# Convolution in groups of five blocks instead of four, with the weights staged in a group buffer and the exponential's table loaded first

## The chip, the core and the metric

The kernel runs on one core of a Trainium2 chip. The core has five engines, each with its own in-order instruction queue: PE (TensorE, matrix products; its weight loads are listed apart as PEld), DVE (VectorE), ACT (ScalarE), POOL (GpSimd) and SP (SyncE, which here only starts DMA transfers). PE writes to PSUM, an accumulator memory of eight banks, and a bank can be used again only after another engine has copied its result out, which is called eviction here. All other operands lie in SBUF, the on-chip working memory. The metric is the device time of one execution in microseconds (us); smaller is better.

## The reference

The computation is a short causal convolution over the sequence followed by a maxout layer. Each of 8 heads (24 of the 192 channels each) has 7 taps, normalised by a softmax; then come three products with 192x768 weights, an elementwise maximum and one product back.

```python
B, S, D = x.shape                 # 8, 4160, 192
w = weight - np.max(weight, axis=-1, keepdims=True)      # 8 heads x 7 taps
w = np.exp(w)
w = w / (np.sum(w, axis=-1, keepdims=True) + 1e-09)
...
out = np.einsum('hk,bskhg->bshg', w, x_unf)              # 7 taps, causal
...
h = np.maximum(np.maximum(x @ w1, x @ w2), x @ w3)       # 768 hidden columns
return (h @ w_out).astype(np.float32)
```

## The kernel before

**Blocks and steps.** The 33,280 tokens are cut into NB = 65 blocks of 512. After a hand-ordered front (lines 677 to 726), the main loop (line 747) runs one step per block t, from 2 to 64. A step does the first layer of block t (`l1`, L503, six columns j of 128 hidden units), the second layer of block t - 1 (`st2`, L567), and feeds later blocks: it loads their rows, casts them, and convolves them.

**The maximum.** The weights are stored as differences w1 - w3 and w2 - w3 (`make_wd`, L302), so a column needs two sets of products, `lp` (PSUM pool psp, two banks) and `lq` (pool psq, two banks). `top` turns them into the hidden value: ACT computes r = relu(lp) (L490), then DVE takes max(r, lq) (L491). The missing w3 part goes straight to the output through a small matrix m16 (`make_m`). The second layer accumulates in `po` (pool psw, four banks), and ACT and DVE add its two halves (L574, L575).

**Two lanes.** Contractions of 192 are cut into pieces of 64 rows, and PE holds two such pieces at a time, one in each half of its rows. The two lanes are queues of recorded products (`mm`, `emit`); `emit` interleaves them by the number of columns that each has streamed. `meet` empties both lanes before work that needs all rows. On the chip the result is one in-order PE queue.

**The convolution.** For block 4 on, the rows of x (fp32, buffers `xf`) are cast by POOL to fp16 into a group tile x16 (`cast_x`, L194), which holds the blocks of a group side by side. `conv` (L357) multiplies them with a band matrix (`band`) built from the 7 taps: for each head, four column blocks and two row halves, a 39x32 product whose width is 48 columns per block of the group: 48 for the single block 4, 96 for the pairs 5 to 12, 192 for the groups of four from block 13 (QUADS) on. The results G use two psw banks, one psp and one psq bank (WPWQ). `evac` (L397) evicts them to `ys`: ACT the two psw banks, then DVE the psp bank and the psq bank. `turn` (L411) transposes two blocks at a time by DMA from SP's queue into a tile `yp`, and `double` (L420, POOL) copies it to the other half of the partitions, since each lane reads its own half.

**When it happens.** `convs_at` names the steps that hold a convolution, called late steps: a pair is convolved in one step, a group of four in two halves of four heads, in the steps t - 4 and t - 3 for a group starting at block t. The burst stands after column j = 1, behind a `meet`. `OWN` and `AHEAD` give the lanes unequal numbers of second-layer products ahead of it, so that both end together. `casts` and `loads` say up to which block a step casts and loads; from block 11 on, the loads use three `xf` buffers in turn.

**The front.** SP issues the loads of block 0, the weights in pieces (`ws`, `w3s`), and blocks 1 to 3. ACT loads the 8x7 taps and computes their exponential (L269), which needs a function table; DVE normalises it into `line` (L274); PE turns `line` into the band (L283), which ACT and DVE evict (L287). Blocks 0 to 3 use another convolution (`conv_dense`, L378) with their rows cast into `xz` (L211), by DVE for block 0, by POOL and ACT for block 1. `keep_warm` (L252) issues products without use, to keep PE active.

Of the kernel before, what the change touches and what calls it, by code (L numbers as in the profile page):

```python
# [10 lines left out]
FP32 = mybir.dt.float32  # L11
FP16 = mybir.dt.float16
AXX = mybir.AxisListType.X
AF = mybir.ActivationFunctionType

P = 128
KW = 7
PAD = KW - 1
NHEAD = 8
GRP = 24  # L20
BAND_W = 128 + PAD
# [7 lines left out]
def kernel(  # L29
# [12 lines left out]
    nc = tc.nc  # L42
# [5 lines left out]
    DFF = moe_w1.shape[1]  # L48
# [9 lines left out]
    for b in range(B):  # L58
        s = nfull * NBLK
        while s < SEQ:  # L60
            n = min(SEQ - s, NBLK - off)
# [8 lines left out]
    NB = len(blocks)  # L70
# [15 lines left out]
    NDENSE = 4  # L86
# [12 lines left out]
    const = ctx.enter_context(tc.tile_pool(name="const", bufs=1))  # L99
    x16p = ctx.enter_context(tc.tile_pool(name="x16p", bufs=2))  # L100
    x16q = ctx.enter_context(tc.tile_pool(name="x16q", bufs=2))
    ysp = ctx.enter_context(tc.tile_pool(name="ysp", bufs=2))
    ydp = ctx.enter_context(tc.tile_pool(name="ydp", bufs=4))
    ypp = ctx.enter_context(tc.tile_pool(name="ypp", bufs=4))
    rp = ctx.enter_context(tc.tile_pool(name="rp", bufs=4))
    hp = ctx.enter_context(tc.tile_pool(name="hp", bufs=2))
    tp = ctx.enter_context(tc.tile_pool(name="tp", bufs=2))
# [2 lines left out]
    psp = ctx.enter_context(tc.tile_pool(name="psp", bufs=2, space=bass.MemoryType.PSUM))  # L110
    psq = ctx.enter_context(tc.tile_pool(name="psq", bufs=2, space=bass.MemoryType.PSUM))
    psw = ctx.enter_context(tc.tile_pool(name="psw", bufs=4, space=bass.MemoryType.PSUM))

    QUADS = 13
    assert (NB - QUADS) % 4 == 0
    xin, xbuf, XBUF, loaded = {}, [], 7, set()

    def get_x(t):
# [52 lines left out]

    pairs = {NDENSE: (NDENSE, 0, 1)}
    for t in range(NDENSE + 1, NB):
        u = (t - NDENSE - 1) % 2 if t < QUADS else (t - QUADS) % 4
        pairs[t] = (t - u, u, 2 if t < QUADS else 4)

    def place(t):
        return pairs.get(t, (t, 0, 0))
# [3 lines left out]
    def cast_x(t):  # L182
        if not 0 <= t < NB:
            return
        xf, p0, _ = xin.pop(t)
        t0, u, nu = place(t)
        if u == 0:
            pool = x16q if nu == 4 else x16p
            x16s[t0] = pool.tile([P, NHEAD, 4, nu, 2, GRP], FP16, tag="x16", name=f"x16_{t0}")
        if p0:  # L190
            nc.gpsimd.memset(xf[0:p0, 0, :], 0.0)
        K = HALF + KR
        for r in range(2):
            nc.gpsimd.tensor_copy(out=x16s[t0][0:K, :, :, u, r, :].rearrange("p h j c -> p j h c"),  # L194
                                  in_=xf[0:K, 4 * r:4 * r + 4, :].rearrange("p j (h c) -> p j h c", c=GRP))

    NC, NSLOT, CYC = D // HALF, D // 32, 96
# [16 lines left out]

    ws = const.tile([P, NC, DFF], FP32)
    w3s = const.tile([P, 2, DFF], FP32)
    PW = 2 * P

    def load_wa(f):
# [6 lines left out]

    wk = const.tile([NHEAD, KW], FP32)
    nc.scalar.dma_start(out=wk[:], in_=weight)  # L230
    wos = const.tile([P, NJ, D], FP32)
    load_x(0)
    load_wa(slice(0, PW))
# [14 lines left out]
    def keep_warm(n, pool=psw, tag="w"):  # L248

        ps = pool.tile([P, NBLK], FP32, tag=tag, name="idle")  # L250
        for _ in range(n):
            nc.tensor.matmul(ps[:], lhsT=idle[:, 0:P], rhs=idle[:], start=True, stop=True)  # L252
# [6 lines left out]
    nc.vector.memset(line[:], 0.0)  # L259
    for v in range(2):  # L260
        nc.vector.memset(xz[0][v][:], 0.0)
    band = const.tile([P, NHEAD, BAND_W], FP16)
    nc.vector.memset(band[:], 0.0)
    keep_warm(5, psp, "p")
    wexp = const.tile([NHEAD, KW + 1], FP32)
    nc.vector.memset(wexp[:], 1e-9)
    wneg = const.tile([NHEAD, 1], FP32)
    nc.vector.reduce_max(out=wneg[:], in_=wk[:], axis=AXX, negate=True)
    nc.scalar.activation(out=wexp[:, 0:KW], in_=wk[:], func=AF.Exp, bias=wneg[:])  # L269
    wrec = const.tile([NHEAD, 1], FP32)  # L270
    nc.vector.reduce_sum(out=wrec[:], in_=wexp[:], axis=AXX)
    nc.vector.reciprocal(out=wrec[:], in_=wrec[:])
# [6 lines left out]
    for lo, hi, copy in ((0, CUT, nc.scalar.copy), (CUT, WIN, nc.vector.tensor_copy)):  # L279
# [6 lines left out]
        for a in range(4):  # L286
            copy(out=band[32 * a:32 * a + 32, :, 32 * a + lo:32 * a + hi],  # L287
                 in_=bps[:, 0:hi - lo, :].rearrange("p c h -> p h c"))
# [102 lines left out]
    def evac(t, i, copy=nc.scalar.copy):  # L391
        if t >= NB:
            return
        G, h0 = convs[t]
        per = G[i].shape[1]
        h0 += per * (i // 2)
        copy(out=slots[t][:, i % 2, :, :, GRP * h0:GRP * (h0 + per)].rearrange(  # L397
                 "p u r (h c) -> p h (u r) c", c=GRP),
             in_=G[i][:].rearrange("p h (n c) -> p h n c", c=GRP))

    def turn(t, vs=(0,)):


        nu = place(t)[2]
        for v in vs:
            n = min(nu, 2)
            yp = ypp.tile([P, 2, 2, n, NC, P], FP16, tag="yp", name=f"yp_{t + v}")
            for u in range(n):
                dense[t + v + u] = yp
            for i in range(2):  # L410
                nc.sync.dma_start_transpose(out=yp[:, 0, i, :, :, :].rearrange("p u k n -> p (u k) n"),  # L411
                                            in_=slots[t][:, i, v:v + n, :, :].rearrange("p u r d -> p (u r d)"))

    def double(t):

        if not NDENSE <= t < NB:
            return
        yp = dense[t]
        for i in range(2):
            nc.gpsimd.tensor_copy(out=yp[HALF * i:HALF * (i + 1), 1, :, :, :, :].rearrange("p i u k n -> p (i u k n)"),  # L420
                                  in_=yp[HALF * (1 - i):HALF * (2 - i), 0, :, :, :, :].rearrange("p i u k n -> p (i u k n)"))

    def spot(t, i, c, r):

        _, u, nu = place(t)
        u, nu = u % 2, min(nu, 2)
        f = NC * (r % 2) + c
        return (((f % 2 != i) * 2 + r // 2) * nu + u) * NC + f // 2

# [27 lines left out]
    def op(fn):  # L457
        ops.append((tuple(put), fn))
# [21 lines left out]
    def meet():  # L480

        emit(True)
        assert not ops
        clock[0] = clock[1] = 0
# [244 lines left out]

    convs_at = {2: 4, 3: 5, 4: 7}  # L730
    convs_at.update({t - 3: t for t in range(9, QUADS, 2)})
    convs_at.update({t - 4 + i: t for t in range(QUADS, NB, 4) for i in range(2)})
    casts = {4: 9}
    for t in range(5, NB):
        casts[t] = min(NB - 1, casts[t - 1] + (2 if t in (6, 7, 8) else 1))
    loads = {t: min(NB - 1, casts.get(t + 1, 0) + (t < 7 or t > 9)) for t in range(4, NB)}
    loads.update({2: 9, 3: 10})

    def load_on(t):
        for v in range(loads[t - 1] + 1, loads[t] + 1):  # L740
            if v not in loaded:
                load_x(v)
# [4 lines left out]
    for t in range(2, NB):  # L747
        u = convs_at.get(t, NB)
        late = t > 2 and u < NB
        if t in (3, 4):  # L750
            double(t + 1)
        if t > 3:
            for v in range(casts.get(t - 1, 8) + 1, casts[t] + 1):
                cast_x(v)
        l1(t, 0)
        if t == 2:
            first_rest()
        elif t == 3:
            cast_x(8)
            nc.gpsimd.tensor_copy(out=m16[0:HALF, 2, :], in_=m16[HALF:P, 0, :])  # L760
            nc.gpsimd.tensor_copy(out=m16[HALF:P, 2, :], in_=m16[HALF:P, 1, :])
        if t > 3 and not late:
            op(lambda t=t: (store(t - 2, 0, 4, (nc.sync,)),
                            turn(t + 2, (2,)) if place(t + 2)[1:] == (0, 4) else None, load_on(t)))
        else:
            op(lambda t=t: store(t - 2, 0, 4, (nc.sync,)))
        cuts = ROOM if late else EVEN
        st2(t - 1, (cuts[0], cuts[0]))
        for j in range(1, NJ):
            l1(t, j)  # L770
            if late and j == 1:
                st2(t - 1, (cuts[0] + OWN + AHEAD, cuts[0] + OWN))
                meet()
                quad, second = u >= QUADS, u < QUADS or t == u - 3
                conv(u, WPWQ, range(4 * second, 4 * second + 4) if quad else range(NHEAD))
                for i in (0, 2):
                    evac(u, i)
                for i in (1, 3):
                    evac(u, i, nc.vector.tensor_copy)
                if second:  # L780
                    turn(u)
                load_on(t)
            if t == 2 and j == 1:
                meet()
                conv_dense(3, (ACT, DVE))
                zero_x(1, NQ, NR, nc.vector)
                cross(3, GP)
                load_x(8)
                cast_x(6)
            elif t == 2 and j == 3:  # L790
                meet()
                conv(u, WW)
                evac(u, 0)
                evac(u, 1, nc.vector.tensor_copy)
                turn(4)
                load_x(9)
                cast_x(7)
            st2(t - 1, (cuts[j], cuts[j]))
            if j == 1 and t > 4 and t + 2 in pairs and pairs[t + 2][1] % 2 == 0:
                double(t + 2)  # L800
            if t == NB - 1 and j == 3:
                op(lambda: store(NB - 2, 0, 2, (nc.sync,)))
        if t == NB - 1:
            op(lambda: store(NB - 2, 2, 4, (nc.sync,)))
# [29 lines left out]
```

## Time and profile before

| | us |
|---|---|
| median of 3 runs | 454.24 |
| lowest and highest run | 454.09, 456.25 |
| the profiled execution: its time | 454.51 |
| the profiled execution: span from the first to the last instruction | 452.7 |

The page that the profiler gives for one execution has busy times per engine, the chain of work that ended last (followed back from the last instruction, at each step to what released it), and the costliest groups of instructions. A group names its source line, engine, operation, the tile written and the tiles read, the shape, how often it ran, its total busy time in us and the mean duration of one in ns; then comes the idle time of the engine just before these instructions and what ended it. A timeline row has the start (us from the first instruction), the duration from the first start to the last end of the merged instructions, and then the same names; in brackets stands the idle time before it and its releaser. Rows of the chain are start, duration, and what ran. Durations of overlapping instructions on one engine include the overlap.

| | before |
|---|---|
| L567, 64x192 second-layer products | 3744, 243 ns each |
| L503, 64x512 first-layer products | 2232, 376 ns each |
| L357, convolution products, width 192, 96, 48 | 832, 256, 64 |
| L397, evictions of 384 columns, ACT | 61, 482 ns each |
| L397, evictions of 384 columns, DVE | 61, 550 ns each |
| L411, DMA transposes on SP's queue | 62, median 1280 ns to issue |
| L420, doublings on POOL: 64x1536, 64x768 | 60 at 1465 ns, 2 at 825 ns |
| L630 and L614, DVE evictions of 192 and 384 columns | 358 and 551 ns |

Each product is listed with its latency; two products of one lane follow each other at a shorter distance than the listed duration.

### The profile page before, as it was taken

What the parts mean: (1) busy time and instruction counts of PE and PEld (TensorE: products, weight loads), DVE (VectorE), ACT (ScalarE), POOL (GpSimd) and SP (SyncE); (2) the same over time, 40 slices, a digit from 0 to 9 for tenths busy, and PEclk for the clock granted to TensorE, in tenths of its full rate; (3) what the DMA queues carried; (4) which work ended last, traced back from release to release, by engine and by line L of the source; (5) the groups of instructions that cost most, each with busy time, mean ns of one, the idle gap of its engine ahead of it and who ended that gap; (6) DMA issues with size and microseconds to landing.
All of it is one profiled execution on the core that took longest, in us unless ns stands there. A gap on an engine that the chain in (4) does not pass through costs nothing.

```text
span 452.7 us, 18493 instructions
## 1 busy us (share of the span) xinstructions
PE 446.8 (99%) x7702; PEld 412.6 (91%) x7702; DVE 356.5 (79%) x617; ACT 320.0 (71%) x604; POOL 202.9 (45%) x226
## 2 busy tenths in 40 slices
PE   7999999999999999999999999999999999999997
PEld 3569999999999999999999999999999999999996
DVE  7768778878878787887878788887878788787775
ACT  7767767767777676777767777776767777776664
POOL 2864836556454534645263464535346452505000
PEclk9999999999999999999999999999999999999999
DMA  7969997596875869587685949657594776535223
GB/s 205 231 178 166 199 205 195 146 206 180 169 180 147 168 129 207 138 176 185 118 190 141 210 117 184 177 136 186 133 206 124 178 189 118 117 89 104 59 72 106
DMA packets 127987, 72.03 MB, mean 159 GB/s; under 512 B 52064, under 2 KB 127711, under 8 KB 127903
## 3 DMA queue, kind: packets, MB, share of 16 engines
q1 hardware_dynamic: 127743, 70.75, 68.3%
q8 instruction: 60, 0.98, 1.0%
q14 instruction: 24, 0.20, 0.1%
q10 hardware_dynamic: 160, 0.10, 0.1%
HBM read 33.28 MB, written 25.56 MB: 130 GB/s over the span
## 4 chain that ended last, share of the span: by engine, by line
PE 97%; ACT 1%; DMA 0%; DVE 0%; issue 0%; ACTq 0%
PE po L567 36%; PE lq L503 31%; PE lp L503 22%; PE G L357 3%; PE lw L526 1%; PE lp L526 1%; PE D L378 1%; PE po L625 0%; PE po L598 0%; DMA wk<-in_weight_dram 0%; PE lq L526 0%; ACT xf L137 0%; ACT band L287 0%; ACT L269 0%; PE pm L337 0%; PE band L283 0%
## 5 line engine op out<-in xcount | busy, mean ns | idle before, releaser
L491 DVE TENSOR_TENSOR h<-r,lq 128x512 f16<-128x512 f16 x384 | 263.0, 686 | 85.1 <-ACT r L490 77.3
L567 PE MATMUL po<-wo,h 64*128 64x192 f16 x3024 | 329.8, 243 | 0.0
L490 ACT ACTIVATE r<-lp 128x512 f16<-128x512 f32 x384 | 229.0, 597 | 114.3 <-PE lp L503 100.8
L503 PE MATMUL lp<-yp,wd 64*128 64x512 f16 x1098 | 295.6, 376 | 0.0
L503 PE MATMUL lq<-yp,wd 64*128 64x512 f16 x1098 | 295.5, 376 | 0.0
L567 PEld LDWEIGHTS <-h 64*128 64x128 f16 x3024 | 240.9, 94 | 6.3 <-issue 4.1
L503 PEld LDWEIGHTS <-wd 64*128 64x128 f16 x2268 | 177.7, 94 | 10.6 <-issue 0.2
L194 POOL CAST x<-xf 103x768 f16<-103x768 f32 x122 | 97.5, 827 | 106.6 <-DMA xf<-in_x_dram 93.0
L567 PE MATMUL po<-m,yp 64*128 64x192 f16 x720 | 141.0, 243 | 0.0
L420 POOL COPY yp<-yp 64x1536 f16<-64x1536 f16 (+1 forms) x62 | 89.6, 1445 | 96.2 <-DMA yp<-ys 75.9
L575 DVE TENSOR_TENSOR o<-a,po 128x384 f32<-128x384 f32 x126 | 69.0, 547 | 0.0
L567 PEld LDWEIGHTS <-yp 64*128 64x128 f16 x720 | 66.3, 94 | 0.5
L574 ACT COPY a<-po 128x384 f32<-128x384 f32 x126 | 59.5, 472 | 0.0
L397 ACT CAST ys<-G 128x384 f16<-128x384 f32 x61 | 26.3, 482 | 9.5 <-PE G L357 9.4
L397 DVE CAST ys<-G 128x384 f16<-128x384 f32 x61 | 31.0, 550 | 0.0
L357 PE MATMUL G<-x,band 39*32 39x192 f16 (+2 forms) x1152 | 17.3, 234 | 0.0
L357 PEld LDWEIGHTS <-band 39*32 39x32 f16 x1152 | 10.7, 91 | 5.2 <-issue 4.7
L503 PE MATMUL lp<-yd,wd 64*128 64x512 f16 x36 | 9.7, 376 | 0.0
L503 PE MATMUL lq<-yd,wd 64*128 64x512 f16 x36 | 9.7, 376 | 0.0
L526 PEld LDWEIGHTS <-wd 128*128 128x128 f16 (+1 forms) x48 | 3.2, 98 | 5.7 <-issue 2.4
L211 POOL CAST xz<-xf 112x160 f16<-112x160 f32 (+2 forms) x15 | 4.1, 319 | 7.7 <-DMA xf<-in_x_dram 7.7
L378 PEld LDWEIGHTS <-xz 112*32 112x32 f16 x320 | 4.6, 107 | 2.7 <-issue 1.0
(74 smaller groups left out, 98.2 us busy)
## 6 DMA issues: line engine op xcount, KB each, us to landing
xf<-in_x_dram SPq DMA_DIRECT2D x113, 234.0 KB
out_dram<-o SPq DMA_DIRECT2D x62, 384.0 KB
xf<-in_x_dram SPq DMA_DIRECT2D x7, 204.8 KB
xf<-in_x_dram SPq DMA_DIRECT2D x3, 420.0 KB
ws<-in_moe_w_dram SPq DMA_DIRECT2D x8, 128.0 KB
yp<-ys SPq DMA_TRANSPOSE x62
out_dram<-o SPq DMA_DIRECT2D x5, 192.0 KB
wos<-in_moe_w_out_dram SPq DMA_DIRECT2D x1, 576.0 KB
```

The costliest lines, as they stand in the source:

```text
L194: nc.gpsimd.tensor_copy(out=x16s[t0][0:K, :, :, u, r, :].rearrange("p h j c -> p j h c"), in_=xf[0:K, 4 * r:4 * r + 4, :].rearrange("p j ( ...
L357: nc.tensor.matmul(G[2 * (k // per) + i][TOK * j:TOK * (j + 1), k % per, :], lhsT=band[row, h, HALF * i + LAP:HALF * i + KR], rhs=x16s[t0] ...
L378: nc.tensor.matmul(ps[32 * g:32 * g + 32, lo:hi], lhsT=xz[t][v][0:rlen, q, 32 * s:32 * s + 32], rhs=band[0:rlen, h, cc:cc + hi - lo], star ...
L397: copy(out=slots[t][:, i % 2, :, :, GRP * h0:GRP * (h0 + per)].rearrange("p u r (h c) -> p h (u r) c", c=GRP), in_=G[i][:].rearrange("p h ...
L420: nc.gpsimd.tensor_copy(out=yp[HALF * i:HALF * (i + 1), 1, :, :, :, :].rearrange("p i u k n -> p (i u k n)"), in_=yp[HALF * (1 - i):HALF * ...
L490: nc.scalar.activation(out=r[:], in_=ps[0][:], func=AF.Relu)
L491: nc.vector.tensor_max(out=hs[t][:, j, :], in0=r[:], in1=ps[1][:])
L503: nc.tensor.matmul(ps[i][:], lhsT=w_of(i, c, j), rhs=y_all(t, i, c), start=(n == 0), stop=(n == NC - 1))
L526: nc.tensor.matmul(open_ps[t, j, i][:], lhsT=a, rhs=b, start=(t, j, i) not in begun, stop=(t, j, i) in begun)
L567: nc.tensor.matmul(ps[b0, i][:, s % 2, :], lhsT=a, rhs=b, start=first, stop=last)
L574: nc.scalar.copy(out=a[:], in_=ps[s - 1, 0][:])
L575: nc.vector.tensor_add(out=outs[t][:, s - 1:s + 1, :], in0=a[:], in1=ps[s - 1, 1][:])
```

## The change

From block 15 on, groups hold five blocks (NU = 5): the products are 240 columns wide and a group tile holds five blocks. Blocks 13 and 14 become a pair, so there are five pairs (5 to 14) and ten groups of five instead of four pairs and thirteen groups of four. A late half now evicts 480 columns per bank. The fifth block of a group is transposed alone, in the step before the group (`turn(t + 1, (4,))`), into a `yp` tile of its own, and doubled alone; `spot` gives its places. `ypp` has five buffers instead of four. Step 9 has no convolution any more and casts two blocks instead of one, and the late steps 9 and 10 of the first group become 11 and 12, behind the pair's step 10.

The staged weights `ws` and `w3s` become slices of one tile `wall`, which is taken from the pool of the group tiles (x16q, two buffers) instead of standing on its own for the whole kernel.

In the front a 1x1 exponential is issued on ACT right behind the load of the taps, so that the function table is loaded there; its DVE memset stands first in DVE's queue. The memset of `band` and the idle products move behind the exponential of the taps.

```diff
--- before.py
+++ after.py
@@ -101,7 +101,7 @@
     x16q = ctx.enter_context(tc.tile_pool(name="x16q", bufs=2))
     ysp = ctx.enter_context(tc.tile_pool(name="ysp", bufs=2))
     ydp = ctx.enter_context(tc.tile_pool(name="ydp", bufs=4))
-    ypp = ctx.enter_context(tc.tile_pool(name="ypp", bufs=4))
+    ypp = ctx.enter_context(tc.tile_pool(name="ypp", bufs=5))
     rp = ctx.enter_context(tc.tile_pool(name="rp", bufs=4))
     hp = ctx.enter_context(tc.tile_pool(name="hp", bufs=2))
     tp = ctx.enter_context(tc.tile_pool(name="tp", bufs=2))
@@ -111,8 +111,8 @@
     psq = ctx.enter_context(tc.tile_pool(name="psq", bufs=2, space=bass.MemoryType.PSUM))
     psw = ctx.enter_context(tc.tile_pool(name="psw", bufs=4, space=bass.MemoryType.PSUM))
 
-    QUADS = 13
-    assert (NB - QUADS) % 4 == 0
+    QUADS, NU = 15, 5
+    assert (NB - QUADS) % NU == 0
     xin, xbuf, XBUF, loaded = {}, [], 7, set()
 
     def get_x(t):
@@ -171,8 +171,8 @@
 
     pairs = {NDENSE: (NDENSE, 0, 1)}
     for t in range(NDENSE + 1, NB):
-        u = (t - NDENSE - 1) % 2 if t < QUADS else (t - QUADS) % 4
-        pairs[t] = (t - u, u, 2 if t < QUADS else 4)
+        u = (t - NDENSE - 1) % 2 if t < QUADS else (t - QUADS) % NU
+        pairs[t] = (t - u, u, 2 if t < QUADS else NU)
 
     def place(t):
         return pairs.get(t, (t, 0, 0))
@@ -185,7 +185,7 @@
         xf, p0, _ = xin.pop(t)
         t0, u, nu = place(t)
         if u == 0:
-            pool = x16q if nu == 4 else x16p
+            pool = x16q if nu == NU else x16p
             x16s[t0] = pool.tile([P, NHEAD, 4, nu, 2, GRP], FP16, tag="x16", name=f"x16_{t0}")
         if p0:
             nc.gpsimd.memset(xf[0:p0, 0, :], 0.0)
@@ -214,8 +214,8 @@
 
 
 
-    ws = const.tile([P, NC, DFF], FP32)
-    w3s = const.tile([P, 2, DFF], FP32)
+    wall = x16q.tile([P, NC + 2, DFF], FP32, tag="x16", name="wall")
+    ws, w3s = wall[:, 0:NC, :], wall[:, NC:NC + 2, :]
     PW = 2 * P
 
     def load_wa(f):
@@ -228,6 +228,9 @@
 
     wk = const.tile([NHEAD, KW], FP32)
     nc.scalar.dma_start(out=wk[:], in_=weight)
+    warm = const.tile([1, 1], FP32)
+    nc.vector.memset(warm[:], 0.0)
+    nc.scalar.activation(out=warm[:], in_=warm[:], func=AF.Exp)
     wos = const.tile([P, NJ, D], FP32)
     load_x(0)
     load_wa(slice(0, PW))
@@ -259,14 +262,14 @@
     nc.vector.memset(line[:], 0.0)
     for v in range(2):
         nc.vector.memset(xz[0][v][:], 0.0)
-    band = const.tile([P, NHEAD, BAND_W], FP16)
-    nc.vector.memset(band[:], 0.0)
-    keep_warm(5, psp, "p")
     wexp = const.tile([NHEAD, KW + 1], FP32)
     nc.vector.memset(wexp[:], 1e-9)
     wneg = const.tile([NHEAD, 1], FP32)
     nc.vector.reduce_max(out=wneg[:], in_=wk[:], axis=AXX, negate=True)
     nc.scalar.activation(out=wexp[:, 0:KW], in_=wk[:], func=AF.Exp, bias=wneg[:])
+    band = const.tile([P, NHEAD, BAND_W], FP16)
+    nc.vector.memset(band[:], 0.0)
+    keep_warm(5, psp, "p")
     wrec = const.tile([NHEAD, 1], FP32)
     nc.vector.reduce_sum(out=wrec[:], in_=wexp[:], axis=AXX)
     nc.vector.reciprocal(out=wrec[:], in_=wrec[:])
@@ -403,7 +406,7 @@
 
         nu = place(t)[2]
         for v in vs:
-            n = min(nu, 2)
+            n = min(nu - v, 2)
             yp = ypp.tile([P, 2, 2, n, NC, P], FP16, tag="yp", name=f"yp_{t + v}")
             for u in range(n):
                 dense[t + v + u] = yp
@@ -423,7 +426,7 @@
     def spot(t, i, c, r):
 
         _, u, nu = place(t)
-        u, nu = u % 2, min(nu, 2)
+        u, nu = u % 2, min(nu - u + u % 2, 2)
         f = NC * (r % 2) + c
         return (((f % 2 != i) * 2 + r // 2) * nu + u) * NC + f // 2
 
@@ -729,10 +732,10 @@
 
     convs_at = {2: 4, 3: 5, 4: 7}
     convs_at.update({t - 3: t for t in range(9, QUADS, 2)})
-    convs_at.update({t - 4 + i: t for t in range(QUADS, NB, 4) for i in range(2)})
+    convs_at.update({t - 4 + i: t for t in range(QUADS, NB, NU) for i in range(2)})
     casts = {4: 9}
     for t in range(5, NB):
-        casts[t] = min(NB - 1, casts[t - 1] + (2 if t in (6, 7, 8) else 1))
+        casts[t] = min(NB - 1, casts[t - 1] + (2 if t in (6, 7, 8, 9) else 1))
     loads = {t: min(NB - 1, casts.get(t + 1, 0) + (t < 7 or t > 9)) for t in range(4, NB)}
     loads.update({2: 9, 3: 10})
 
@@ -761,7 +764,8 @@
             nc.gpsimd.tensor_copy(out=m16[HALF:P, 2, :], in_=m16[HALF:P, 1, :])
         if t > 3 and not late:
             op(lambda t=t: (store(t - 2, 0, 4, (nc.sync,)),
-                            turn(t + 2, (2,)) if place(t + 2)[1:] == (0, 4) else None, load_on(t)))
+                            turn(t + 2, (2,)) if place(t + 2)[1:] == (0, NU) else None,
+                            turn(t + 1, (4,)) if place(t + 1)[1:] == (0, NU) else None, load_on(t)))
         else:
             op(lambda t=t: store(t - 2, 0, 4, (nc.sync,)))
         cuts = ROOM if late else EVEN
```

## The prediction

> **What bounds the kernel now.** I read the page's busy table and its chain of waits first, then the costliest groups, then the timeline of one convolution half and of the front.
>
> ```profile
> PE 446.8 (99%) x7702; PEld 412.6 (91%) x7702; DVE 356.5 (79%) x617; ACT 320.0 (71%) x604; POOL 202.9 (45%) x226
> PE 97%; ACT 1%; DMA 0%; DVE 0%; issue 0%; ACTq 0%
> ...
> 211.16 0.45 PE G L357 x32
> 218.09 0.46 PE G L357 x32
> 237.74 0.46 PE G L357 x32
> ```
>
> PE (the tensor engine) is busy 99% of the span and carries 97% of the chain; no other engine holds it up for long. So a gain must shorten PE's stream, and a loss must make PE wait. The last three lines, from the chain in order of time, are three convolution halves (L357). The first two lie one step apart: 6.93 us. Between the second and third lie three steps, one of which contains a half: 19.65 us. Subtracting, a plain step takes (19.65 - 6.93)/2 = 6.36 us and a half adds 0.57 us.
>
> ```profile
> 210.92 0.24 PE L567 MATMUL po<-m,yp 64*128 64x192 f16 x1
> 211.09 0.53 PE L357 MATMUL G<-x,band 39*32 39x192 f16 x32
> 211.55 0.25 PE L567 MATMUL po<-wo,h 64*128 64x192 f16 x1
> 211.65 0.41 PE L567 MATMUL po<-wo,h 64*128 64x192 f16 x3
> ...
> 211.25 0.69 DVE L491 TENSOR_TENSOR h<-r,lq 128x512 f16<-128x512 f16 x1 [0.37 <-ACT r L490]
> 211.51 0.86 ACT L397 CAST ys<-G 128x384 f16<-128x384 f32 x2 [0.30 <-PE G L357]
> 211.85 1.01 DVE L397 CAST ys<-G 128x384 f16<-128x384 f32 x2
> 211.99 0.37 PE L503 MATMUL lq<-yp,wd 64*128 64x512 f16 x1
> 212.96 0.38 PE L503 MATMUL lq<-yp,wd 64*128 64x512 f16 x1
> ...
> L397 DVE CAST ys<-G 128x384 f16<-128x384 f32 x61 | 31.0, 550 | 0.0
> L383 DVE CAST yd<-D 128x512 f16<-128x512 f32 x3 | 2.1, 692 | 1.7 <-PE D L378 1.6
> ```
>
> This is the half at 211 us: the burst of 32 products, the two evictions each on ACT and DVE, and the first `lq` products of the next two columns. The two psq banks alternate, so the `lq` at 212.96 reuses the bank that the second DVE eviction empties.
>
> ```profile
> 2.50 1.28 ACT L269 ACT_TABLE_LOAD   x1 [2.50 <-DMA wk<-in_weight_dram]
> 4.50 0.22 DVE L274 TENSOR_SCALAR line<-wexp,wrec 8x7 f16<-8x7 f32 x1
> 7.29 1.91 PE L378 MATMUL D<-band,xz 112*32 112x103 f16 x80
> 9.39 0.86 POOL L211 CAST xz<-xf 112x160 f16<-112x160 f32 x3 [7.72 <-DMA xf<-in_x_dram]
> 10.96 1.11 PE L378 MATMUL D<-band,xz 112*32 112x103 f16 x80
> ```
>
> At the front PE waits for the band, which waits for the exponential's table; later it waits for block 1's rows.
>
> **Fewer bursts.** A quad or quintet needs two halves of 32 products, a pair one burst of 64. Before: 13 groups, 26 halves. After: 10 groups, 20 halves, and one more pair (block 13). In a half eight products run side by side (two row halves, four column blocks), four rounds. Three 192-column products span 0.41 us and one lasts 0.24, so they follow each other after (0.41 - 0.24)/2 = 0.085 us; four rounds are 0.34 of the 0.57, and 0.23 is the price of leaving and re-entering the normal stream. A 512-column product follows after 0.215 us (the `lp` rows at 211.64, 211.86, 212.07), so a column costs (0.215 - 0.085)/320 = 0.41 ns, and 48 more columns in four rounds cost 0.08 us. A wider half is 0.65. The added pair costs 0.79: the chain has bursts at 71.16 (a pair) and 78.31, one step and one pair apart, 7.15 - 6.36. Sum: 20 x 0.65 + 0.79 - 26 x 0.57 = -1.03 us. This lies on the path.
>
> **Wider evictions, the term that works against it.** Each DVE eviction grows from 384 to 480 elements. No row has 480; by the 512 row a column costs (692 - 550)/128 = 1.11 ns, so +0.106 us each and +0.21 for the two, which run back to back and begin when the maximum before them ends, as now. Now they end at 211.85 + 1.01 = 212.86; a bank is usable about 0.05 later (the maximum ends at 211.94, `lq` starts at 211.99), 212.91, and PE comes for it at 212.96. After: ready at 213.12, PE comes 0.08 later than now, 213.04: a wait of 0.08. In the second half (evictions 218.78 + 1.02, `lq` at 219.88) it is 220.06 against 219.96. I take 0.09. Behind the waiting `lq` stands all of PE's queue, in order; PE has no idle time in which to make it up, so it reaches the next step: 20 x 0.09 = +1.8 us. Bounds: 0 if something absorbs it; with the price per column of 1.005 ns from L630 and L614 (192 and 384 columns, 358 and 551 ns) the wait is about 0.07, with 1.11 at most 0.11, so 1.4 to 2.2. ACT's evictions grow by about 0.08 each (482 and 587 ns at 384 and 512); the bank of the second is then free at 212.6 and wanted at 212.88: hidden. Next in line is `lq` of the column after, which waits for a maximum delayed by 0.1 and comes 0.17 later itself: no second wait.
>
> [...]
>
> **The early table.** The load needs nothing but ACT, which is free at 1.33 (its weight DMA issue, 0.58 from 0.75): it ends at 2.61 instead of 3.78, the 1x1 exponential adds 0.2 to 0.3 (the real one takes 0.30), the real one ends near 3.15 instead of 4.10. The band's memset, 0.51 on DVE, is now behind the maximum (about 2.65 to 3.16) and beside that. `line` is ready 0.95 earlier, and so are the band and block 0's products. But block 1's rows land when they did: POOL casts them 9.39 to 10.25, so the products of 10.96 start at about 10.29: 0.67 gained. PE is slow at first (80 such products take 1.91 at 7.29, 1.11 at 10.96). If full speed comes at about 10.96 as now, 0.67 us of them run slowly and lose 0.67 x (1 - 1.11/1.91) = 0.28. I take -0.4. Bounds: -0.67, and +0.13 if all 80 run slowly (1.91 - 1.11 - 0.67). Behind them POOL's weights (L302, 13.40 onwards, waiting for DMA) come in time by 0.2 us or more.
>
> [...]
>
> **What costs nothing, and its cover.** Weights in a group buffer: the order of instructions shows the same waits; the last reader of the staged weights (L310) ends at 17 us, the first cast that takes that buffer is block 20's near 90. Ten more transposes on SP's queue (62 to 72, 1.28 us each): a group's last block is transposed in the step before the group and doubled two steps into it, 12 us of cover; stores and loads behind it move by 2.6 us once in five steps, against casts some 8 us ahead of their use. POOL: 25 pair doublings and 11 single ones instead of 30 and 1, 2 x (11 x 0.825 - 5 x 1.465 - 0.825) = +1.9 us in all, at 45% busy.
>
> **Sum.** -1.03 + 1.8 - 0.4 = +0.4 us. The profiled execution took 454.51 (span 452.7), 0.27 above the median 454.24 and inside its runs' 454.09 to 456.25. Applied to the median: **454.6**. Its own range, by the bounds: -1.03 + 1.4 - 0.67 to -1.03 + 2.2 + 0.13, 453.9 to 455.5.
>
> **Rivals.** A, the wait is absorbed: the eviction stays in the shade and only the switches and the front count, 454.24 - 1.03 - 0.4 = 452.8. For it: PE comes 0.08 later, which eats part. Against: now the margin is just 0.05.
>
> B, slower, at the handover from pairs to quintets. The cast of block 19 must precede the first wide half in step 11 at about 91.8 us (85.23, the burst of step 10, less 0.57, plus 7.15), and one more cast (two in step 9) is squeezed in:
>
> ```profile
> 80.53 1.59 POOL L194 CAST x<-xf 103x768 f16<-103x768 f32 x2 [5.00 <-DMA xf<-in_x_dram]
> 94.41 1.60 POOL L194 CAST x<-xf 103x768 f16<-103x768 f32 x2 [7.57 <-DMA xf<-in_x_dram]
> ```
>
> POOL would run casts 17 and 18, a doubling (2.99) and cast 19: 80.53 + 1.6 + 1.6 + 3.0 + 1.6 = 88.4, 3.4 spare. With a wait of 7.57 like the second row's before the last, it ends at 96 and PE stands 4 us; I price it at 3: 457.6. It decides once that cast ends after 91.8.
>
> C, the table load isn't really moved: front gain 0, 455.0. Against: it stands first on ACT, without a wait.
>
> **Chances.** Forecast 0.48, A 0.28, B 0.18, C 0.06. A measurement can't tell a change under 0.5%, 2.27 us (451.97 to 456.51). All gains together (-1.03 - 0.67) stay inside; I leave 0.14, out of A, for more than I can price. Slower by more: B and a little of the rest, 0.19. Same: 0.67. The range reaches to 452.0 and 457.0.
>
> **What would show it.** L357's busy time for a wide half 0.53 to 0.6 and steps with a half 7.1 us long instead of 6.93 (rival A: 7.01); `lq` starting 0.05 after the second DVE eviction; that eviction near 655 ns; `line` near 3.8 us and block 1's products near 10.3; POOL's cast of block 19 ending before 92. I am wrong if PE waits for POOL anywhere, or if the bank is free before PE asks.

## The result, and the profile after

The changed kernel takes 457.11 us (median of 19 runs, 455.10 to 460.44), the kernel before 454.61 (19 runs, 453.66 to 456.99). The ratio of the two is 1.0053, 95% interval [1.0038, 1.0068]: 2.5 us between the medians, and beyond the 457.0 that the range reached to. The profiled execution of the changed kernel took 457.96, span 456.2 us against 452.7. Lines of the code behind L233 stand three higher than before (L378 is now L381, L357 is L360, L503 is L506, L420 is L423). Of all runs below, four were slowed as a whole (one each of e1, e11 and e16, and one of the kernel before beside e17); the medians hold them, the ratios leave them out.

The busy table and the DMA queues of the changed kernel (packets, MB, share of 16 engines):

```profile
PE 447.7 (98%) x7574; PEld 408.3 (90%) x7574; DVE 357.0 (78%) x608; ACT 319.1 (70%) x595; POOL 204.6 (45%) x236
...
q1 hardware_dynamic: 128063, 70.75, 76.2%
```

The same queue in the kernel before:

```profile
q1 hardware_dynamic: 127743, 70.75, 68.3%
```

PE is busy 0.9 us longer (447.7 instead of 446.8), in a span that is 3.5 us longer: most of the loss is in stretches where PE stands. And the same 70.75 MB occupy the DMA engines for 76.2% of the span instead of 68.3%. The trace's packet records say which packets are slower: those of 768 bytes (rows of x and of the output) take 52.3 ns on the mean instead of 46.3.

What PE waited for from 12 us on, changed kernel (us in total, times, longest):

```profile
PE D L381 <- issue: 1.6, 1, 1.6
PE G L360 <- issue: 1.5, 3, 0.9
PE lq L506 <- POOL yp L423: 0.3, 1, 0.3
```

The page calls it "issue" when an engine waited for nothing that the profile shows. The longest stretch, in the chain of waits (start, us), and the same place in the kernel before:

```profile
26.87 0.89 PE D L381 x58
27.76 1.60 issue
29.36 0.34 PE D L381 x13
```

```profile
27.38 0.90 PE D L378 x59
28.28 0.40 issue
28.68 0.34 PE D L378 x13
```

Before, the same products stood only 0.40 us, at the same place in the stream (after the 67th product in the timeline). The last line of the list above is a wait for a doubling on POOL that came late. POOL at the handover from pairs to groups of five, changed kernel:

```profile
84.38 1.59 POOL L194 CAST x<-xf 103x768 f16<-103x768 f32 x2 [5.37 <-DMA xf<-in_x_dram]
87.56 1.59 POOL L194 CAST x<-xf 103x768 f16<-103x768 f32 x2 [1.59 <-DMA xf<-in_x_dram]
89.21 2.99 POOL L423 COPY yp<-yp 64x1536 f16<-64x1536 f16 x2
92.27 1.60 POOL L194 CAST x<-xf 103x768 f16<-103x768 f32 x2
```

The casts of blocks 17 and 18 wait for their rows, and the doubling of blocks 11 and 12 stands behind them. The cast of block 19 ends at 93.87; the first wide half, which needs it, starts at 94.29.

The wide halves of the convolution run near the forecast. Three of them in the chain, and the evictions of the third with the `lq` product that needs the bank:

```profile
161.20 0.53 PE G L360 x32
168.28 0.54 PE G L360 x32
194.37 0.54 PE G L360 x32
```

```profile
195.05 1.22 DVE L400 CAST ys<-G 128x480 f16<-128x480 f32 x2
...
196.32 0.37 PE L506 MATMUL lq<-yp,wd 64*128 64x512 f16 x1
```

Five blocks take 194.37 - 161.20 = 33.17 us, 6.634 a block; before, four took 237.74 - 211.16 = 26.58, 6.645 a block.

The front: the table load, the finished taps and block 1's products.

```profile
1.38 1.28 ACT L233 ACT_TABLE_LOAD   x1 [1.38 <-PEq L822]
3.47 0.22 DVE L277 TENSOR_SCALAR line<-wexp,wrec 8x7 f16<-8x7 f32 x1
10.12 1.30 PE L381 MATMUL D<-band,xz 112*32 112x103 f16 x80 [0.32 <-POOL xz L211]
```

All three are earlier, by 1.12, 1.03 and 0.84 us. Block 3's products start at 26.87 in the chain, still 0.51 us ahead of before (27.38); past the stretch, at 29.36, PE is 0.68 behind (28.68).

### The profile page after: what moved, and what is told of

Same layout as the page of the kernel before. It is cut to its first block, busy times and chain, and to the rows that moved or that the text cites. A ratio compares the mean times of both kernels' runs of the same rounds, so it can differ in the third digit from the quotient of the medians.

```text
span 456.2 us, 18270 instructions
## 1 busy us (share of the span) xinstructions
PE 447.7 (98%) x7574; PEld 408.3 (90%) x7574; DVE 357.0 (78%) x608; ACT 319.1 (70%) x595; POOL 204.6 (45%) x236
## 3 DMA queue, kind: packets, MB, share of 16 engines
q1 hardware_dynamic: 128063, 70.75, 76.2%
## 4 chain that ended last, share of the span: by engine, by line
PE 94%; DMA 2%; issue 1%; POOL 1%; DVE 1%; ACT 0%; SPq 0%; ACTq 0%; POOLq 0%
PE po L570 35%; PE lq L506 30%; PE lp L506 21%; PE G L360 3%; DMA xf<-in_x_dram 2%; PE D L381 1%; PE lw L529 1%; POOL yp L423 1%; PE lp L529 1%; PE po L628 0%; PE po L601 0%; SPq L164 0%; PE idle L255 0%; PE band L286 0%; PE pm L340 0%
## 5 line engine op out<-in xcount | busy, mean ns | idle before, releaser
L506 PE MATMUL lp<-yp,wd 64*128 64x512 f16 x1098 | 295.9, 376 | 0.1
L506 PE MATMUL lq<-yp,wd 64*128 64x512 f16 x1098 | 295.5, 376 | 0.3 <-POOL yp L423 0.3
L506 PEld LDWEIGHTS <-wd 64*128 64x128 f16 x2268 | 183.3, 94 | 17.4 <-issue 0.7
L423 POOL COPY yp<-yp 64x1536 f16<-64x1536 f16 (+1 forms) x72 | 91.4, 1270 | 81.0 <-DMA yp<-ys 67.1
L400 ACT CAST ys<-G 128x480 f16<-128x480 f32 (+1 forms) x51 | 25.4, 544 | 11.2 <-PE G L360 11.1
L400 DVE CAST ys<-G 128x480 f16<-128x480 f32 (+1 forms) x51 | 30.0, 628 | 0.7 <-PE G L360 0.7
L360 PE MATMUL G<-x,band 39*32 39x240 f16 (+2 forms) x1024 | 16.9, 242 | 1.5 <-issue 1.5
L360 PEld LDWEIGHTS <-band 39*32 39x32 f16 x1024 | 10.3, 91 | 6.3 <-issue 5.8
L506 PE MATMUL lq<-yd,wd 64*128 64x512 f16 x36 | 9.8, 376 | 0.0
L506 PE MATMUL lp<-yd,wd 64*128 64x512 f16 x36 | 9.7, 376 | 0.0
L381 PEld LDWEIGHTS <-xz 112*32 112x32 f16 x320 | 4.7, 108 | 4.2 <-issue 2.2
```

The source lines that it names most:

```text
L360: nc.tensor.matmul(G[2 * (k // per) + i][TOK * j:TOK * (j + 1), k % per, :], lhsT=band[row, h, HALF * i + LAP:HALF * i + KR], rhs=x16s[t0] ...
L381: nc.tensor.matmul(ps[32 * g:32 * g + 32, lo:hi], lhsT=xz[t][v][0:rlen, q, 32 * s:32 * s + 32], rhs=band[0:rlen, h, cc:cc + hi - lo], star ...
L506: nc.tensor.matmul(ps[i][:], lhsT=w_of(i, c, j), rhs=y_all(t, i, c), start=(n == 0), stop=(n == NC - 1))
```

## The experiments

Each kernel was timed beside runs of the kernel before on the same chip. "Move" is how far the x tiles of the loop stand from their place in the kernel before, counted from multiples of 256 bytes in a partition (staging the weights in a group's buffer moves them by 60 x 256 bytes, counted as 0). "768 B" is the mean time of such a packet; "idle" sums PE's idle stretches over 0.1 us after 12 us, both from the one profiled execution (that of e11 isn't read).

| run | kernel | move, bytes | median, before | ratio [95%] | 768 B, ns | idle, us |
|---|---|---|---|---|---|---|
| - | before | 0 | 454.61 | | 46.3 | 0.4 |
| - | changed | 32 | 457.11, 454.61 | 1.0053 [1.0038, 1.0068] | 52.3 | 3.5 |
| e1 | front edit alone | 32 | 456.15, 454.67 | 1.0034 [1.0015, 1.0053] | 51.1 | 0.6 |
| e2 | groups of five alone | 0 | 454.31, 454.67 | 0.9986 [0.9961, 1.0011] | 48.9 | 0.7 |
| e3 | staged weights alone | 0 | 454.70, 454.67 | 1.0000 [0.9986, 1.0014] | 47.0 | 0.9 |
| e4 | changed, again | 32 | 456.89, 454.67 | 1.0051 [1.0024, 1.0078] | 53.8 | 2.7 |
| e5 | changed, tile of 64 | 64 | 456.17, 454.43 | 1.0039 [1.0022, 1.0055] | 52.4 | 1.1 |
| e6 | before, moved | 32 | 456.16, 454.43 | 1.0039 [1.0019, 1.0060] | 51.9 | 3.1 |
| e7 | front edit, tile of 64 | 64 | 455.26, 454.43 | 1.0018 [1.0002, 1.0034] | 50.3 | 1.7 |
| e8 | groups of five, moved | 32 | 457.42, 454.43 | 1.0052 [1.0024, 1.0080] | 52.8 | 3.6 |
| e9 | changed, tile of 128 | 128 | 455.22, 454.42 | 1.0016 [0.9998, 1.0035] | 50.3 | 0.4 |
| e10 | front edit, tile of 128 | 128 | 455.33, 454.42 | 1.0020 [1.0004, 1.0035] | 46.7 | 1.1 |
| e11 | before, x tiles moved, those behind by 128 | 32 | 457.59, 454.42 | 1.0064 [1.0043, 1.0084] | | |
| e12 | before, tiles behind x moved by 32 | 0 | 454.66, 454.42 | 1.0009 [0.9998, 1.0020] | 47.3 | 1.8 |
| e13 | changed, no tile moved | 0 | 454.62, 454.61 | 0.9998 [0.9974, 1.0022] | 48.2 | 0.5 |
| e14 | front edit, no tile moved | 0 | 454.94, 454.61 | 1.0001 [0.9982, 1.0020] | 46.8 | 1.0 |
| e15 | e13, block 6 loaded later | 0 | 454.54, 454.61 | 0.9998 [0.9976, 1.0021] | 48.1 | 0.2 |
| e16 | changed, block 6 loaded later | 32 | 457.53, 454.61 | 1.0050 [1.0023, 1.0077] | 51.8 | 2.3 |
| e17 | before, moved | 128 | 455.34, 454.45 | 1.0020 [1.0001, 1.0039] | 48.2 | 1.5 |
| e18 | before, moved | 256 | 454.80, 454.45 | 1.0006 [0.9994, 1.0019] | 47.2 | 0.6 |

**Which part costs it (e1 to e4).** Each part of the diff alone, and the changed kernel again. The first is the kernel before with the lines from `warm` on and the new place of `band`; the second is the rest of the diff; the third only this:

```diff
-    ws = const.tile([P, NC, DFF], FP32)
-    w3s = const.tile([P, 2, DFF], FP32)
+    wall = x16q.tile([P, NC + 2, DFF], FP32, tag="x16", name="wall")
+    ws, w3s = wall[:, 0:NC, :], wall[:, NC:NC + 2, :]
```

> The kernel before with the front edit alone (early exponential, 1x1 tile, order of the band's memset); groups of four, weights in tiles of their own. Theory 'the front gives nothing back' (my prediction): 0.4 us faster, 454.2; line near 3.5 us, burst of the second block pair 0.4 to 0.7 us earlier, and PE's longest idle stretch behind 20 us still 0.4 us. Theory 'the front gain turns into a stall before the products of block 3': a stretch of about 1.6 us in which PE waits for nothing near 28 us (0.4 us before), and a time of 454.6 to 455.8, that is 0 to 1.2 us slower. If the stall belongs to the other edits it is absent here.

> The changed kernel without the front edit: groups of five, staged weights, casts. Theory 'eviction waits' (my prediction): +0.8 us over before, 455.4, no idle time of PE between 84 and 105 us. Theory 'handover' (late casts at the change from pairs to groups): 1.5 to 2.5 us slower, 456.1 to 457.1, with PE stretches of 0.3 to 1 us at 85 to 103 us that wait for POOL or follow a doubling, and with steady steps that cost only 0.68 us a half.

> The kernel before with one edit: the weights staged in a group's buffer, which moves the x tiles by 15 KB in each partition. Theory 'place in SBUF slows the transfers': the 768-byte packets of the queue that loads x take 52 ns on the mean instead of 46 and the time goes up by 0.5 to 2 us. Theory 'staging costs nothing' (my prediction): 454.2 to 454.8 and 46 ns, and the slow packets belong to the one execution of the changed kernel that was profiled.

> The changed kernel once more, beside the three above on one chip. 456.5 to 457.5 expected from its 19 runs. If slow packets are an accident of the profiled execution, this profile has 46 ns for the 768-byte packets and no stretch of 0.9 us at 87 us; if they come with the kernel, it has 52 ns and the stretch again.

My own theory of the trace, that the loss came with the groups of five at the handover, fell: e2 isn't slower. The cheap front edit is the slow part (1.5 us), and by neither mechanism expected of it: its stretch at block 3 was 0.5 us. What the slow kernels share is the packets, 51 ns and more. What the front edit has that the others lack is a new tile: `warm` holds 4 bytes, takes 32 in each partition, and everything allocated behind it moves by 32. In the compiled programs the three x tiles of the loop start at bytes 72960, 79104 and 100992 before, and at 57632, 63776 and 85664 in the changed kernel: remainders by 64 of 0 and of 32.

**The tile or the early table (e5 to e8).** The tile at 64 bytes, and the move without the edit:

```diff
# e5, e7
-    warm = const.tile([1, 1], FP32)
+    warm = const.tile([1, 16], FP32)
# e6, e8
-    wk = const.tile([NHEAD, KW], FP32)
+    wks = const.tile([NHEAD, 16], FP32)
+    wk = wks[:, 0:KW]
```

> The changed kernel with one size changed: the tile of the early exponential is 64 bytes in each partition instead of the 32 that its 4 bytes are rounded to, so that every tile behind it (x, staged rows, outputs) starts where it does in the kernel before, counted from multiples of 64 bytes; instructions are the same. Theory 'the 32-byte shift slows the transfers': 768-byte packets fall from 53 ns (median 38) to 46 to 49 ns (median 36), the stretches of PE at 87 to 102 us are gone, and the time is 453 to 454.3, that of groups of five alone (454.31) less up to 1 us of front. Theory 'the earlier front makes the transfers collide': no difference, 456.5 to 457.2.

> The kernel before, with the tile of the raw weights made 64 bytes in each partition instead of 32: the same instructions, every later tile 32 bytes further. Theory 'the 32-byte shift': 768-byte packets 50 to 52 ns, median 38, and 1 to 2 us slower than before, 455.7 to 456.7. Theory 'the earlier front': no difference, 454.4 to 454.9.

> The front edit alone with its tile at 64 bytes. Theory 'the 32-byte shift': median packet 36 ns and 0.3 to 1 us faster than before, 453.7 to 454.4, the front's own gain without its side effect. Theory 'the earlier front': like the front edit with the small tile, 456.

> Groups of five and staged weights without the front edit, every later tile moved by 32 bytes. Theory 'the 32-byte shift': median packet 38 ns and as slow as the changed kernel or slower, 456.5 to 457.5. Theory 'the earlier front': 454.3 as without the shift.

e6 and e8 settle half of it: with no edit but 32 unused bytes the kernel before loses 1.7 us, and groups of five are at 457.42 instead of 454.31 (3.0 us above the runs beside them). But 64 bytes didn't mend it, against what was expected of e5 and e7.

**128 bytes, and whose place it is (e9 to e12).** The tile at 128 bytes (`[1, 32]`); and the kernel before with the last x tile made longer, so that the loop's x tiles and all in front of them are moved by 32 and what lies behind by 128 (e11), or only what lies behind, by 32: cast rows, staged rows, transposed rows, outputs (e12).

```diff
# e11: the weights' tile at 64 bytes as in e6, and 96 bytes behind the last x tile; e12: 32 bytes there alone
+            if t < XBUF - 1:
...
+                xl = const.tile([P, NR * D + 24], FP32, name=f"xf_{t}")
+                xbuf.append(xl[:, 0:NR * D].rearrange("p (q d) -> p q d", d=D))
```

> The changed kernel with the tile of the early exponential at 128 bytes in each partition: every later tile stands as in the kernel before counted from multiples of 128 bytes (with 64 it did so only from multiples of 64, and the packets stayed slow). Theory 'starts off multiples of 128 bytes slow the transfers': 768-byte packets 46 to 49 ns, median 36; 453.3 to 454.3, faster than before by 0.2 to 1 us. Theory 'the early front itself makes it slow': median 38 and 456 to 457.

> The front edit alone with its tile at 128 bytes. Theory 'starts off multiples of 128': median packet 36 ns, 453.6 to 454.3, faster than before by 0.2 to 0.8 us, the front's own gain. Theory 'the early front itself': 455 to 456.

> The kernel before with the x tiles moved by 32 bytes (the raw weights' tile at 64 bytes) and everything behind them (cast rows, staged rows, outputs) moved back to a multiple of 128 by 96 bytes more in the last x tile. Theory 'the loads of x suffer': 4-byte packets (transposes) stay at 10.2 ns, 768-byte packets rise part of the way to 52, and most of the 1.7 us of the run with everything moved, 455.4 to 456.2. Theory 'stores and transposes suffer': 454.4 to 454.9.

> The kernel before with the x tiles where they are and everything behind them (cast rows, staged rows, outputs) moved by 32 bytes (32 bytes more in the last x tile). Theory 'the loads of x suffer': 454.4 to 454.9, 4-byte packets 11.3 ns. Theory 'stores and transposes suffer': 455.4 to 456.2, and the 768-byte mean between 46 and 52.

So it is the x tiles: with them 32 bytes off the loss is 3.2 us, and with only the tiles behind them 32 bytes off nothing can be measured (0.2 us, interval -0.1 to +0.9). e11 is not quite the x tiles alone, for the tiles behind stand 128 bytes off in it; their part was not tried apart, but with everything moved by 128 (e17 below) the whole loss is 0.9 us. With 128 bytes (e9, e10) 0.8 to 0.9 us remain, which was not expected of the theory; the interval of e9 just holds zero.

**No move at all, and one load out of the way (e13 to e16).** The early exponential's value in the weights' own 32-byte row, and a load moved:

```diff
# e13, e14, e15
-    wk = const.tile([NHEAD, KW], FP32)
+    wks = const.tile([NHEAD, KW + 1], FP32)
+    wk, warm = wks[:, 0:KW], wks[0:1, KW:KW + 1]
-    warm = const.tile([1, 1], FP32)
# e15, e16
-    for t in range(NDENSE, XBUF):
+    for t in range(NDENSE, XBUF - 1):
         load_x(t)
...
+    load_x(6)
     load_x(7)
```

> The changed kernel with the early exponential's one value in the unused last 4 bytes of the weights' own 32-byte row: no tile is moved at all against groups of five alone. Theory 'place': 453.3 to 454.3, 0.2 to 1 us faster than before, what groups of five alone gave (454.31) and some of the front's 0.6 us. Theory 'the earlier front runs into the late instruction fetch of block 3's products': 454.8 to 455.6 as with 128 bytes, PE idle there for 0.5 us or more in most runs.

> The front edit alone, no tile moved. Theory 'place': 453.6 to 454.2. Theory 'late fetch': 454.6 to 455.5, the 0.6 us gained at block 1's products lost again before block 3's last products, where PE waits for nothing that the profile shows.

> As e13, and the load of block 6 is issued at the end of the opening, beside that of block 7, instead of with those of blocks 4 and 5. Theory 'late fetch': the instruction transfer that came at 25.5 to 27 us comes at about 23.5, PE has no idle stretch before block 3's last products, and the time is 0.5 to 1.5 us below e13 (453 to 454). Theory 'place': no difference to e13; the load may come late for POOL's cast of block 6 instead, then up to 1 us slower.

> The changed kernel as it is (x tiles moved by 32 bytes) with the later load of block 6. If most of its 2.5 us are lost before block 3's last products and in the halved clock behind a long stall there, 455 to 455.6; if they are lost later as well (pair bursts at 58 to 75, handover at 85 to 100 us), 456 to 457 still.

e13 is the answer: the whole change, with the x tiles where e2 has them, takes 454.62 against 454.61. What PE waited for in it after 12 us, and POOL at the handover:

```profile
PE D L381 <- issue: 0.5, 1, 0.5
```

```profile
82.07 1.59 POOL L194 CAST x<-xf 103x768 f16<-103x768 f32 x2 [5.23 <-DMA xf<-in_x_dram]
84.84 1.59 POOL L194 CAST x<-xf 103x768 f16<-103x768 f32 x2 [1.18 <-DMA xf<-in_x_dram]
86.49 2.98 POOL L423 COPY yp<-yp 64x1536 f16<-64x1536 f16 x2
89.54 1.59 POOL L194 CAST x<-xf 103x768 f16<-103x768 f32 x2
```

Every line stands 2.3 to 2.7 us earlier than in the changed kernel, and PE waits for none. The stretches over 0.1 us fall from 3.5 to 0.5 us, 3.0 of the 3.6 us between the spans of these two executions (456.2 and 452.6). The later load of block 6 did nothing for the time with or without the move (e15 454.54 beside e13's 454.62; e16 457.53 beside the changed kernel's 457.11). In the profiled executions the stretch at block 3 is absent in e15 but 2.3 us long in e16, so that load alone is not what holds PE up there.

**128 against 256 (e17, e18).** The kernel before with the weights' tile at 160 and 288 bytes (`[NHEAD, 40]`, `[NHEAD, 72]`).

> The kernel before with the x tiles and everything behind them moved by 128 bytes, nothing else. Theory 'only the place within 128 bytes counts': 454.4 to 454.9, median packet 36 ns, 4-byte packets 10.2 to 10.6 ns. Theory 'multiples of 256 count': 455.1 to 455.6, as e9 and e10.

> The kernel before with the same tiles moved by 256 bytes. Both theories: 454.4 to 454.9 and median 36 ns. If this too is at 455 or more, any move counts, and the place within 128 or 256 bytes isn't the reason.

128 bytes cost 0.9 us, near e9 and e10; for 256 (454.80 against 454.45) the interval holds zero. Every distance from multiples of 128 is the same in both, so 128 is probably not the unit; but the intervals of the two (0.01 to 0.39% and -0.06 to 0.19%) overlap, and that 256 is the unit isn't shown. Of the three x tiles 72960 and 79104 start at multiples of 256, 100992 is 128 off: one of three is off in the kernel before, two after a move by 128, all after 32 or 64. The times go the same way on the whole (-0.4 to 0.4; 0.8 to 0.9; 0.8 to 3.2 us). But what such a start changes in a transfer, no run shows. Whether a kernel with all three tiles at multiples of 256 is faster still was not tried.

## Why the prediction was wrong

**The step that failed** is the early table, and with it "what costs nothing". I priced the 1x1 exponential's instructions and not its tile. It put every x tile 32 bytes off, and my cover for the handover ("casts some 8 us ahead of their use") was taken at the old pace of the loads. The cost is the whole loss: 2.5 us as changed (457.11 - 454.61), none that can be measured without the move (e13, interval -1.2 to +1.0).

**How the slow loads reach PE** is seen in the traces, not tried apart. The instruction queue q8 brings 16 KB at a time, in 60 transfers before and 59 after. The traces hold 15441 instructions of PE before and 15190 after (products, weight loads and a few that handle semaphores), which is 60 and 59 times 256 and a rest: one transfer fits 256 of PE's instructions. And if they are counted in the order of their starts, each of the 27 stretches over 0.1 us called "issue" (after 12 us, in the 19 executions read here) begins when 961, 1217, 2241, 2753 or another number that is 193 more than a multiple of 256 have started. So PE stands where one piece of its instructions ends and the next begins. Around block 3's products, times in us from the span's start:

```
run   q8 transfer      PE goes on   PE stood
e13   25.44 to 26.64   28.30        0.50
e3    26.08 to 27.42   28.79        0.88
e17   26.61 to 27.82   29.34        1.54
after 26.43 to 27.78   29.36        1.60
e6    27.21 to 28.57   30.04        1.89
e16   27.14 to 28.53   29.91        2.30
```

PE goes on 1.3 to 1.7 us after that transfer has ended, in each run that has a stretch there, and where it ended before 25.8 (e2, e5, e9, e12, e15) it didn't stand. In e14 and e18 it ended at 26.73 and 27.36, and PE, which came there only at 28.82 and 29.30, didn't stand either. So PE waits for its own instructions, as far as traces can show it; a burst of short products uses them up fast (block 3's 80 products and as many weight loads take 1.2 us where PE doesn't stand). The page counts x and the instructions on the same 16 DMA engines; that the slower packets of x hold the instructions up is argued, not shown, and single executions vary (e5 is moved too and has the transfer at 24.00 to 24.94). The stretches in the pair bursts at 58 to 75 and at 87 us end the same way: in the changed kernel PE goes on at 58.99 and 86.99, 1.39 and 1.58 us after transfers that ended at 57.59 and 85.41.

**Fewer bursts** was right: a wide half's products take 0.53 to 0.54 us in the chain instead of 0.45 to 0.46, the 0.08 more that was forecast. **Wider evictions** was mis-sized. The DVE pair takes 1.22 instead of 1.01 us, 0.21 more as forecast, ends at 196.27, and `lq` starts 0.05 after it. But only one half of a group waits for it. Both have `lq` 0.05 after the pair's end; the second half of another group:

```profile
168.21 0.60 PE L360 MATMUL G<-x,band 39*32 39x240 f16 x32
168.89 1.22 DVE L400 CAST ys<-G 128x480 f16<-128x480 f32 x2
170.16 0.37 PE L506 MATMUL lq<-yp,wd 64*128 64x512 f16 x1
```

Here `lq` starts 1.95 us after the burst's first product, which is the 1.87 of before (212.96 - 211.09) and the 0.08 of the wider burst: PE comes just then by itself. In this group's first half it is 2.02 us (161.13 to 163.15), 0.07 of waiting. In e13 it is the second half that waits. By the period, a half costs (33.17 - 5 x 6.36)/2 = 0.685 us, against (26.58 - 4 x 6.36)/2 = 0.57 before and the forecast's 0.65 without a wait. The term is 20 x 0.035 = 0.7 us instead of 1.8. Bursts and evictions together: 20 x 0.685 + 0.79 - 26 x 0.57 = -0.3 us; e2 measured -0.4, with an interval from -1.8 to +0.5.

**The front** was right up to block 3: block 1's products start 0.84 us earlier and take 0.19 longer (0.67 and 0.28 in the forecast), and 0.51 us are left at 26.87, against the 0.4 of the forecast. But the instruction transfer did not come earlier with PE: it ended at 27.78 in the changed kernel and at 27.10 in the kernel before, and the gain went at block 3. In the time of e14 it isn't seen (interval -0.8 to +0.9 us); in its profiled execution PE lost 0.87 us at 20.97 to a cast on POOL that waited for its weights.

**The rivals.** A, the absorbed wait, holds for half of the halves. B, the handover, came true by its own mark (the cast of block 19 ended at 93.87, after 91.8), but through slow loads, and PE waited 0.3 us for POOL, for a doubling, instead of 3. Its price of 457.6 lies near the measured time by luck. Without the move (e13) that cast ends at 91.13 and nothing waits, but the burst that needs it starts at 91.57: 0.44 us are spare, not the 3.4 of the forecast, which had the cast end at 88.4. C fell: the table is loaded 1.12 us earlier. Staged weights cost nothing that can be measured (e3, 454.70 against 454.67). So 454.6 is the time of the change without its moved tiles (e13, 453.4 to 455.6 by its interval). That this is the forecast's number is partly luck: with the wait at its measured size the sum would have been -0.3 - 0.4, 453.9 from 454.61, which that interval holds too.

No version here beats the kernel before by more than can be measured; e2 (454.31 against 454.67) is the nearest.

## What to carry to other kernels

Here a new tile of 4 bytes moved every tile allocated behind it by 32: compare the start addresses of what the DMA writes before and after an edit, as one compares the instructions. Moves by 32 and 64 bytes cost 0.8 to 3.2 us in these runs, moves by 128 bytes 0.8 to 0.9, a move by 256 none that could be measured (0.35 us, interval -0.3 to +0.9). The transfers take 68.3% of the span in the kernel before, and a few ns a packet were felt: with 52.3 ns for a packet of 768 bytes instead of e13's 48.2, POOL had the rows of block 18 only at 87.56 instead of 84.84, and PE stood for 3.5 us instead of 0.5, as argued above mostly for its own instructions. The early exponential's value in a word that a tile left unused cost nothing measurable (e13, interval -1.2 to +1.0 us).

## What the hardware showed unexpectedly

In two of the profiled executions a stretch in which PE stood was followed by a lower granted clock, 0.61 and 0.56. In e6 (lines one higher than before: L378 is L379), the chain of waits around block 3 and the window view (for each engine the busy time and the number of instructions; then the granted clock, third from the end, the DMA share and GB/s):

```profile
27.04 0.21 PE lp L504
...
27.25 0.90 PE D L379 x57
28.15 1.89 issue
30.04 0.34 PE D L379 x13
...
31.25 0.42 PE lp L504
```

```profile
26.00:30.00 4.00, 2.15 (x87) 1.45 (x84) 1.84 (x3) 1.96 (x4) 2.84 (x5) 1.00 0.97 209
30.00:34.00 4.00, 3.96 (x45) 2.06 (x44) 2.47 (x4) 1.08 (x2) 2.19 (x3) 0.61 0.52 152
```

After 1.89 us of standing the products follow each other at 0.42 instead of 0.21 us, and the clock is 0.61 over the next 4 us; by these numbers that costs about 4 x 0.39 = 1.6 us more, an estimate. In e8 a stretch of 1.88 us at 72.22 does the same (0.56 over 3.9 us). But 1.91 us in e4 and 2.30 in e16, at block 3, leave it at 1.00. So the length of the stretch doesn't decide it: of these four, the two followed by the lower clock are the shorter ones. What does, no run here shows. Of the changed kernel's 19 runs 5 have a mean clock of 0.995 or 0.996, among them the four longest (458.15 to 460.44); of the kernel before it is 6 of the 149 runs beside e1 to e18. What preceded it in those runs isn't recorded.
